# DeltaNet with an MLP on one core: inverse matrices stored turned over, the preparation of four steps moved into the regular loop, and the opening order written anew

## The chip, the cores and the metric

The kernel runs on one core of a Trainium2 chip. The core has five engines with an instruction queue each: TensorE (PE: matmuls and transposes by matmul; its weight loads are shown as PEld), VectorE (DVE), ScalarE (ACT), GpSimd (POOL) and SyncE (SP, which here only issues DMAs). The metric is the time of one execution on the device in microseconds. Every time below without a unit is in microseconds.

## The reference

Two parts, all in f32. The first is DeltaNet, a linear attention with a state, for 4 batches, 8 heads, 768 tokens and a head dimension of 48:

```python
k_n = k / (np.linalg.norm(k, axis=-1, keepdims=True) + 1e-06)
for t in range(S):
    kt, vt, bt = (k_n[:, :, t], v[:, :, t], beta[:, :, t, None])
    y[:, :, t] = np.einsum('bhd,bhde->bhe', q[:, :, t], state)
    v_old = np.einsum('bhde,bhd->bhe', state, kt)
    state = state + bt[:, :, :, None] * np.einsum('bhd,bhe->bhde', kt, vt - v_old)
```

The second is an MLP on the 3072 tokens so made, with 384 features, 2048 hidden units and 384 outputs: `h = x @ w_in`, `g = h * clip(h + 3, 0, 6) / 6`, `out = g @ w_out`. The weights `w_in` and `w_out` arrive as float64, the rest as float32.

## The kernel before, in words

**Steps.** The 768 tokens are cut into N = 24 chunks of 32, called steps here. One step has all batches and heads: 4 × 32 tokens on the 128 partitions, 8 heads side by side. Inside a chunk the recurrence is solved at once: with L the strictly lower part of beta · k kᵀ, one needs the inverse of I + L, a 32 × 32 triangular matrix for each batch and head, 32 of them a step. The steps are grouped: group 0 is step 0, group 1 steps 1 to 4, group 2 steps 5 to 8, group 3 steps 9 to 12, and so on, four steps and so 128 matrices a group.

**What a step runs.** `norms` (a square on ACT or POOL, a sum on DVE, a root on ACT, four small DVE operations; the last writes `inv`, L410) gives the norms of k. `prep(t)` scales k on POOL (kb, L480), makes the masks mb with beta (L458) and bkb (L468) on POOL, turns k and q by eight PE transposes (pt, L496), copies them with ACT (KQ, L504), multiplies them on PE (sc, L517) and masks the products with DVE into L and LB (L528). `chain(t)` is the recurrence: PE multiplies the state with k and q (ks, L776), DVE forms R (L789), PE multiplies R with the inverse X (pz, L797), ACT copies that to Z, PE forms the update of the state (su, L894), and DVE takes it from the state (L909). An output part makes y, turns it on PE (yt, L842), and ACT writes it as xT (L846), the input of the MLP.

**The inverses.** Step 0 alone is inverted by matmuls (`product`: pi, L566, with DVE transposes and sums between). For the other groups DVE transposes L so that each of the 128 matrices lies on one partition (`taken`, A<-L, L448), eliminates in place (pairs of a product pr and a difference A, L729 and L734, 60 operations; items called `i2` and so on), and transposes back (`given`, X<-A, L452). Group 1 eliminates only the two 16 × 16 halves of each matrix (`halves_of`, L700 and L705, 28 operations) and joins them step by step with matmuls (`join`, L654 and DVE's L664 to L672; word `x`).

`problems` says how a matrix of 32 × 32 lies in the 1024 elements of its partition: element (i, c) of the transpose goes to place 32 c + i. `turn` is the view of L or X that the DVE transposes read or write: per element i, all 4 × 8 places (t, h), so that neighbours of one 32-block lie 32 elements, 128 bytes, apart.

**The weights.** The 16 pieces of w_in and w_out of 768 KB are loaded as bit patterns of float64 and converted: four ACT operations a piece for the exponent (`scales`, L335; word `a`), three DVE operations (`convert`, L357, L362, L368; word `c`).

**The MLP.** A block is two steps, 256 tokens; there are 12. `up` is 16 units per block: three matmuls (ph, L948), a relu on ACT (L956, words `r`) and on DVE a minimum and product into g (L959, words `g`). For block 0 it is done for each of its steps apart (words `ua`, `ub`, 128 tokens wide). `down` multiplies g with w_out (po, L988); from block 2 on it is done with seven products for eight (L1053), with DVE sums of g (L1039).

**The order.** The engines take their instructions in the order in which the program issues them, and that order is written by hand. `ORDER` (L22 to L44) is a string of words; each word takes the next item of one generator, and `w*3` three of them: `k`, `q`, `v`, `w` loads of keys, queries, values and weight pieces, `B` beta, `z` and `s` settings (beta turned by L234, then eye, blocks, corner, places, L252), `n` norms, `p` prep, `m` mask, `b` bkb, `x` product or join, `h` chain, `y` output, `i1`, `i2` items of the inverses of groups 1 and 2, `u` MLP units, `e` output stores. Each load is four DMAs of 48 KB on SP's queue. Two PSUM pools turn over in rings, of two and of four tiles.

After ORDER comes the regular part, a loop over t = LS = 5 to 23. Each step takes NU = 15 MLP units, and `plan` says which item of the chain of step t, and of the preparations of later steps, is issued at which unit. `LA` = 6 is how far the preparation is ahead: step t finishes the preparation of t + 6 (`now`) and begins that of t + 7 (`later`). ORDER therefore holds preparations 0 to 10 and the first item of 11. `fill` gives two or three items a unit of the norms or the next group's inverse; the inverse of group g + 1 is begun in the second step of group g (i == 1) at unit 6, and units 6 to 11 of that step take none of it beyond the first.

Of the kernel before, what the change touches and what calls it, by code (L numbers as in the profile page):

```python
# [22 lines left out]
k*3 B k B*3 z n0*3 w z*3 s z q*2 n0 q n0 q v n0 w n0 a p0 a p0 s p0*2 m0 k*2 w p0 a*3 p0 a c a c v  # L23
p0 x0 a c k a x0*4 k a k x0 c k w*2 n1 c a c*2 k a x0 a*2 k a x0 k c*2 x0*2 n1 v c n1 k a q n2 c w
x0 a x0*2 k*2 m1 a*3 n1 s n2 c n1 a*2 x0 n1 c k*2 x0 n1 v x0 b0 n2 p1 c a n2 s b1 q h0 a c*2 h0 c
n2 w n2 a m2 k h0 s n2 q c z k q p1 n4 a y0 a p1 n2*2 p2*2 h0 q a p1 s*2 q*2 n4 p3 w q c n4 p2 c
p1 n4*2 p3 c n4 q*2 n4 b2 c a p2 p3 q*2 p2 p1 a q p2 c q*2 a p2 k p3 a p3 p4*3 q k m3 p4*2 s p1 p3
v p4 c y0 w y0*2 p3 ua m4 p4 ra ua b4 ua i1*6 ra*2 i1 k w ga i1*2 a ga ua ra i1*2 ua ga*2 i1 ra q
ua v ra a ua v i1 ga i1 ra ga ua s q i1*2 ua i1 ga i1 ra*2 ga i1 a i1*3 h1 ua i1 ra ga v ua ra
i1*2 v a ga i1*2 ga ua ra i1*2 ua a ga y1 i1 ua i1 x1 w x2 ra ua x2 x1 x2 ra ga*2 a x1 ra x1 k x1  # L30
ua x3 k x3 c x1 ra h1 y1 c h1*2 v y1 ga y1*2 q x3 c*2 w x3 a*2 y1 ub a v ub c ga h1 c rb*2 ub q rb
x2*2 k gb*2 v h1 ub q gb ub*2 rb c h2 n5 gb rb h2 gb k x2 ub a m5 v rb gb rb ub c gb y2 ub h2 q rb
w ub gb rb v n5 y2 u gb ub x4 a h2 k*2 q rb q n5 k*2 a n5 a k c rb y2 h2 y2 k gb a k n5 a ub gb y2
h2 ub c rb gb h3 rb ub gb v y2 c k q n5 v x3 h3 x3 y3 k*2 w k h3 a h3 b3 n5 u y3 rb x4 y3 a k n5*2
a w gb y3 c ub k n5 y3*2 rb gb c v n5 c u n5 u h3 ru gu a ru n5 a gu p5 h3 n9 x4 v c p5 b5 u p5 u
a*2 q h4 a p6 p5 a p5 x4 u v ru k c u a ru gu y4 n9 b6 x4 m6 v c q h4 k q gu u x4 k y4 p6 p7 u q
k*3 p6 k p7 h4 k n9 a q h4 p8 p7 p5 a c p5 k u n9 k p7 ru gu h4 p6 p7 m7 n9 h4 q b7 q u a c p6 n9
u p8 ru gu u k c k v n9*2 p8 c n9 b8 n9*3 p6 p8 w u n9 p6 c p8 p7 p8 p7 p9 ru m8 u p8 gu u c q ru
ub gu rb y4 v m9 m10 a i2*3 gb i2*2 k u i2 y4 a i2*3 u i2 k i2 v*2 u a ru*2 gu p10 p9 b10 k b9 p9
q i2 u p10 i2*2 u k i2*2 p10 q i2 v q i2 p9 i2 q a gu p9 q i2 u ru i2 q i2*3 u ru i2*3 p9 c v i2*2  # L40
gu u gu i2*3 v p9 i2*2 u q i2 u ru i2 k q*2 i2 k u gu k i2 u q u ru u i2 gu e v p11 y4 e i2*2 ru
i2 k u i2 u gu u p10 e u p10 i2 p10 e i2*4 y4 u q i2*2 k i2 k i2*2 k i2*5 k i2 ru k gu i2 k i2*2
k*2 p10
# [4 lines left out]
def kernel(  # L48
# [395 lines left out]
    def problems(A):  # L444
        return A.rearrange("p (c i) -> p i c", i=C)
# [239 lines left out]
    def halves_of(g):  # L685

        n = 128
        needs(*(("L", first(g) + i) for i in range(size(g))))
        At = work.tile([128, C + 1, C], FP32, name="A", bufs=1)
        flat = At[:].rearrange("p c i -> p (c i)")  # L690
        A = flat[:, 0 : C * C]
        taken(g, A)
        yield
        D2 = flat.rearrange("p (k r) -> p k r", k=2)[:, :, 0 : HC * C]
        D2 = D2.rearrange("p k (c i) -> p k c i", i=C)
        for j in range(1, HC - 1):
            w = HC - 1 - j
            pr = work.tile([128, C * C // 4 - C // 2], FP32, name="pr", bufs=1)
            pv = pr[0:n, 0 : 2 * j * w].rearrange("p (k c i) -> p k c i", k=2, c=j)
            nc.vector.tensor_tensor(  # L700
                out=pv, in0=D2[:, :, j, j + 1 : HC].unsqueeze(2).to_broadcast([n, 2, j, w]),
                in1=D2[:, :, 0:j, j].unsqueeze(3).to_broadcast([n, 2, j, w]), op=ALU.mult,
            )
            yield
            nc.vector.tensor_tensor(  # L705
                out=D2[:, :, 0:j, j + 1 : HC], in0=D2[:, :, 0:j, j + 1 : HC], in1=pv,
                op=ALU.subtract,
            )
            yield
        nc.vector.memset(A[:, 0 : C * C : C + 1], -1.0)  # L710
        yield 1
        given(g, A)
        past.update(("halves", first(g) + i) for i in range(size(g)))
        yield

    def inverse(g):
# [8 lines left out]
        for j in range(1, C - 1):  # L725
            w = C - 1 - j
            pr = work.tile([128, C * C // 4 - C // 2], FP32, name="pr", bufs=1)
            pv = pr[0:n, 0 : j * w].rearrange("p (c i) -> p c i", c=j)
            nc.vector.tensor_tensor(  # L729
                out=pv, in0=A[:, j, j + 1 :].unsqueeze(1).to_broadcast([n, j, w]),  # L730
                in1=A[:, 0:j, j].unsqueeze(2).to_broadcast([n, j, w]), op=ALU.mult,
# [3 lines left out]
                out=A[:, 0:j, j + 1 :], in0=A[:, 0:j, j + 1 :], in1=pv, op=ALU.subtract  # L735
# [426 lines left out]
    LA = 6  # L1162
    LS = G0 + GS
# [10 lines left out]
    def chain_of(t):  # L1174
        return made(("h", t), lambda: chain(t))
# [54 lines left out]
    def do(word):  # L1230
# [10 lines left out]
        else:  # L1241
            name, t = word[0], int(word[1:])
            if name == "p" and t >= LS + LA:
# [5 lines left out]
    with tc.manual_schedule():  # L1249
# [12 lines left out]
        for t in range(LS, N):  # L1262
            g, i = group(t)
            ch, now, later = chain_of(t), prep_of(t + LA), prep_of(t + LA + 1)
# [18 lines left out]
            }  # L1283
            for u in range(NU):
# [3 lines left out]
                if u == 6 and i == 1:  # L1288
# [9 lines left out]
                if i == 1 and 5 < u < 12:  # L1298
                    continue
# [34 lines left out]
```

## Time and profile before

| what | value |
|---|---|
| time, median of 3 runs | 689.57 (689.39 to 689.74) |
| the profiled execution, own time | 690.61 |
| its span in the profile | 688.9 |
| mean granted PE clock in it | 0.99 |
| HBM read, written | 26.84 MB, 4.72 MB |
| PE instructions | 11208 matmuls, 11208 weight loads |

The costliest groups of the page; after the bar stand busy time, the mean of one in ns, and the idle time of the engine just ahead of them with what ended most of it:

```profile
L948 PE MATMUL ph<-xT,w_in 128*128 128x256 f32 (+1 forms) x1248 | 270.0, 369 | 4.2 <-DVE g L959 2.9
...
L959 DVE SCALAR_TENSOR_TENSOR g<-g,ph 128x256 f32<-128x256 f32 (+1 forms) x208 | 81.0, 396 | 106.0 <-ACT g L956 105.8
...
L1053 PE MATMUL po<-w_out,g 128*128 128x192 f32 x640 | 113.3, 328 | 0.0
...
L734 DVE TENSOR_TENSOR A<-A,pr 128x30 f32<-128x30 f32 (+9 forms) x150 | 54.2, 361 | 3.7
L335 ACT ACTIVATE spare<-spare,places 128x768 uint16<-128x768 uint16 (+1 forms) x56 | 52.5, 940 | 4.1 <-DVE places L252 3.3
L729 DVE TENSOR_TENSOR pr<-A 128x30 f32<-128x30 f32 (+9 forms) x150 | 50.3, 335 | 3.0
...
L480 POOL TENSOR_TENSOR kb<-kf,inv 128x384 f32<-128x384 f32 x24 | 21.6, 900 | 158.4 <-DVE inv L410 73.7
```

### The profile page before, as it was taken

To read this page: it belongs to the slowest core of one execution; us is meant where nothing else is said; L and a number is where in the kernel's file an instruction comes from. 1 tells how busy PE (TensorE), PEld (TensorE's weight loads), DVE (VectorE), ACT (ScalarE), POOL (GpSimd) and SP (SyncE) were. 2 spreads that over 40 slices of the span, in tenths; PEclk is the share of its full clock that TensorE was granted. 3 is DMA by queue.
4 is the path that set the end of the run, shared out by engine and by line. 5 is a ranking of instruction groups with operands and counts; after the bars stand their busy time and mean duration, and the time that the engine had idled before them with its cause. 6 is when DMAs were issued, how large, how long until landed. Compare 5 with 4: busy or idle time off the path is not lost.

```text
span 688.9 us, 25309 instructions
## 1 busy us (share of the span) xinstructions
PE 644.7 (94%) x11208; PEld 565.0 (82%) x11208; DVE 464.3 (67%) x1210; ACT 239.1 (35%) x476; POOL 92.9 (13%) x147
## 2 busy tenths in 40 slices
PE   1468799999999999999999999999999999999997
PEld 1357687767678988988988988988988989989997
DVE  4798776799836986845986745985546985445242
ACT  4886378542132232232232232232232132132220
POOL 5063003331501100501100402100000000000000
PEclk9999799999999999999999999999999999999999
DMA  9877026402132030031020030020020020000000
GB/s 236 240 184 183 4 83 134 83 3 58 29 60 46 3 65 9 3 73 33 4 59 14 3 70 2 3 59 2 3 48 2 2 48 2 25 3 1 25 0 24
DMA packets 88494, 33.20 MB, mean 48 GB/s; under 512 B 80160, under 2 KB 83232, under 8 KB 88384
## 3 DMA queue, kind: packets, MB, share of 16 engines
q1 hardware_dynamic: 88128, 31.29, 19.9%
q8 instruction: 88, 1.44, 0.9%
q10 hardware_dynamic: 256, 0.30, 0.2%
q14 instruction: 22, 0.18, 0.1%
HBM read 26.84 MB, written 4.72 MB: 46 GB/s over the span
## 4 chain that ended last, share of the span: by engine, by line
PE 76%; DVE 14%; DMA 4%; issue 2%; SPq 2%; ACT 1%; POOL 0%; DVEq 0%; ACTq 0%
PE ph L948 33%; PE po L1053 21%; PE po L988 5%; PE ks L776 3%; PE pz L797 3%; DVE A L734 3%; PE pt L496 3%; PE su L894 2%; PE py L797 2%; DVE pr L729 2%; DVE g L1039 2%; PE sc L517 2%; DMA vf<-in_v_dram 1%; PE yt L842 1%; DVE R L789 1%
## 5 line engine op out<-in xcount | busy, mean ns | idle before, releaser
L948 PE MATMUL ph<-xT,w_in 128*128 128x256 f32 (+1 forms) x1248 | 270.0, 369 | 4.2 <-DVE g L959 2.9
L948 PEld LDWEIGHTS ph<-xT,w_in 128*128 128x128 f32 x1248 | 220.2, 192 | 33.9 <-DVE g L959 4.7
L956 ACT ACTIVATE g<-ph,halves 128x256 f32<-128x256 f32 (+1 forms) x208 | 94.8, 457 | 201.7 <-PE ph L948 200.9
L959 DVE SCALAR_TENSOR_TENSOR g<-g,ph 128x256 f32<-128x256 f32 (+1 forms) x208 | 81.0, 396 | 106.0 <-ACT g L956 105.8
L1053 PE MATMUL po<-w_out,g 128*128 128x192 f32 x640 | 113.3, 328 | 0.0
L1053 PEld LDWEIGHTS po<-w_out,g 128*128 128x128 f32 x640 | 103.8, 190 | 0.5
L1053 PE MATMUL po<-spare,g 128*128 128x192 f32 x480 | 84.8, 330 | 0.0
L1053 PEld LDWEIGHTS po<-spare,g 128*128 128x128 f32 x480 | 78.1, 190 | 1.8
L1039 DVE TENSOR_TENSOR g<-g 128x256 f32<-128x256 f32 x160 | 65.5, 463 | 0.5 <-PE po L1053 0.5
L734 DVE TENSOR_TENSOR A<-A,pr 128x30 f32<-128x30 f32 (+9 forms) x150 | 54.2, 361 | 3.7
L335 ACT ACTIVATE spare<-spare,places 128x768 uint16<-128x768 uint16 (+1 forms) x56 | 52.5, 940 | 4.1 <-DVE places L252 3.3
L729 DVE TENSOR_TENSOR pr<-A 128x30 f32<-128x30 f32 (+9 forms) x150 | 50.3, 335 | 3.0
L988 PE MATMUL po<-w_out,g 128*128 128x384 f32 x128 | 45.7, 493 | 0.0
L1060 ACT ACTIVATE o<-po 128x192 f32<-128x192 f32 x40 | 13.2, 330 | 88.1 <-PE po L1053 88.1
L480 POOL TENSOR_TENSOR kb<-kf,inv 128x384 f32<-128x384 f32 x24 | 21.6, 900 | 158.4 <-DVE inv L410 73.7
L458 POOL TENSOR_TENSOR mb<-beta_tok,mask 128x256 f32<-128x256 f32 x48 | 34.5, 741 | 47.2 <-DVE LB L528 47.1
L504 ACT ACTIVATE KQ<-pt 128x512 f32<-128x512 f32 x48 | 28.3, 595 | 35.0 <-PE pt L496 34.6
L846 ACT ACTIVATE xT<-yt 128x384 f32<-128x384 f32 x24 | 11.7, 487 | 64.3 <-PE yt L842 64.3
L988 PEld LDWEIGHTS po<-w_out,g 128*128 128x128 f32 x128 | 22.9, 190 | 11.9
L496 PE MATMUL pt<-ident,kb 128*128 128x128 f32 x96 | 16.2, 295 | 14.7 <-POOL kb L480 14.5
L909 DVE TENSOR_TENSOR state<-state,su 128x384 f32<-128x384 f32 x46 | 23.2, 546 | 9.7 <-PE su L894 9.7
L789 DVE SCALAR_TENSOR_TENSOR y<-ks,parity,y 128x192 f32<-128x192 f32 x46 | 17.0, 412 | 17.6 <-ACT y L813 17.6
(109 smaller groups left out, 601.3 us busy)
## 6 DMA issues: line engine op xcount, KB each, us to landing
kf<-in_k_dram SPq DMA_DIRECT2D x96, 48.0 KB, 2.5
qb<-in_q_dram SPq DMA_DIRECT2D x96, 48.0 KB, 2.3
vf<-in_v_dram SPq DMA_DIRECT2D x96, 48.0 KB, 2.1
out_dram<-o SPq DMA_DIRECT2D x92, 48.0 KB, 1.6
spare<-in_moe_w_in_dram SPq DMA_DIRECT2D x4, 768.0 KB, 5.9
w_out<-in_moe_w_in_dram SPq DMA_DIRECT2D x4, 768.0 KB, 5.8
w_out<-in_moe_w_out_dram SPq DMA_DIRECT2D x4, 768.0 KB, 5.8
spare<-in_moe_w_out_dram SPq DMA_DIRECT2D x4, 768.0 KB, 4.6
```

Of the source, the lines that this page charges most:

```text
L335: nc.scalar.activation(out=z, in_=z if n else d.bitcast(I16)[:, :, :, 3], func=func, bias=places[:, n : n + 1], scale=scale,)
L458: nc.gpsimd.tensor_tensor(out=mb[:, e], in0=beta_tok[:, t, e:H:2].unsqueeze(2).unsqueeze(3).to_broadcast([P, NP, 2, C]), in1=mask2[:].unsq ...
L496: nc.tensor.transpose(pt[:, p, :], src[:, 2 * p : 2 * p + 2].rearrange("p e w -> p (e w)"), ident[:])
L729: nc.vector.tensor_tensor(out=pv, in0=A[:, j, j + 1 :].unsqueeze(1).to_broadcast([n, j, w]), in1=A[:, 0:j, j].unsqueeze(2).to_broadcast([n ...
L734: nc.vector.tensor_tensor(out=A[:, 0:j, j + 1 :], in0=A[:, 0:j, j + 1 :], in1=pv, op=ALU.subtract)
L797: nc.tensor.matmul(ps[rows(place(b)), D * h : D * h + D], lhsT=m(h)[rows(b)], rhs=z[rows(b), D * h : D * h + D], start=True, stop=True, sk ...
L948: nc.tensor.matmul(ph[:, cols], lhsT=w_in[:, s, f * 128 : (f + 1) * 128], rhs=xT[:, s, cols], start=(s == 0), stop=(s == NKT - 1),)
L956: nc.scalar.activation(out=g, in_=ph, func=ACTF.Relu, bias=half, scale=1.0 / 6.0)
L959: nc.vector.scalar_tensor_tensor(out=g, in0=g, scalar=1.0, in1=ph, op0=ALU.min, op1=ALU.mult)
L988: nc.tensor.matmul(pos[c][:], lhsT=gs[blk, f // 2][:, f % 2, c * P : (c + 1) * P], rhs=w_out[:, f, :], start=(f == 0), stop=(f == NFC - 1),)
L1039: nc.vector.tensor_tensor(out=A(f, *out), in0=A(f, *a), in1=A(f, *b), op=op)
L1053: nc.tensor.matmul(ps[n][:], lhsT=A(f - f % 2, *a)[:, f % 2], rhs=b[:, f], start=(f == 0), stop=(f == HF - 1),)
```

## The change

Three things are done.

1. `problems` gives element (i, c) the place 32 i + c, so the 1024 elements of a matrix are written by A<-L and read by X<-A in sequence. The L and X sides of the two transposes stay as they were. `halves_of` and `inverse` index A with the two axes exchanged: the same number of operations on the same number of elements.

2. `LE = 4`: ORDER holds preparations 0 to 8 and the first item of 9. The loop makes up for it: at t = 5 it issues 9 and 10 and begins 11, at t = 6 it issues 11 and 12 and begins 13; from t = 7 on it is as before. The additional one (`more`) is taken at units 7, 8 and 10 to 13. The inverse of group 3 is begun at t = 7, unit 0, not at t = 6, unit 6, without the skipped units; those of later groups are begun as before.

3. ORDER is written anew: 786 words' worth of items for 804. The number of MLP units, chain, output and inverse items in it is the same. Among what differs: SP issues eight loads of k and four of q ahead of the first weight piece, where four of k stood ahead of it; the small DVE operations of the first norms stand ahead of the transpose of beta; of group 1 only step 1 is joined between X<-A and the next MLP unit; and parts of the preparations of 5 to 7 stand ahead of the first unit of block 1.

The core of the diff, without the text of ORDER beyond its first lines:

```diff
 ORDER = """
-k*3 B k B*3 z n0*3 w z*3 s z q*2 n0 q n0 q v n0 w n0 a p0 a p0 s p0*2 m0 k*2 w p0 a*3 p0 a c a c v
+k*3 B z k B k*4 B q B n0*7 q*3 w n1 z n1 k s p0 z k z n1 m0 w n1 p0*3 s p0*2 n1*2 z k q n1 k a*3
...
     def problems(A):
-        return A.rearrange("p (c i) -> p i c", i=C)
+        return A.rearrange("p (i c) -> p i c", c=C)
...
             nc.vector.tensor_tensor(
-                out=pv, in0=A[:, j, j + 1 :].unsqueeze(1).to_broadcast([n, j, w]),
-                in1=A[:, 0:j, j].unsqueeze(2).to_broadcast([n, j, w]), op=ALU.mult,
+                out=pv, in0=A[:, j + 1 :, j].unsqueeze(2).to_broadcast([n, w, j]),
+                in1=A[:, j, 0:j].unsqueeze(1).to_broadcast([n, w, j]), op=ALU.mult,
             )
             yield
             nc.vector.tensor_tensor(
-                out=A[:, 0:j, j + 1 :], in0=A[:, 0:j, j + 1 :], in1=pv, op=ALU.subtract
+                out=A[:, j + 1 :, 0:j], in0=A[:, j + 1 :, 0:j], in1=pv, op=ALU.subtract
             )
...
     LA = 6
+    LE = 4
...
-            if name == "p" and t >= LS + LA:
+            if name == "p" and t >= LS + LE:
                 next(prep_of(t), None)
...
-            ch, now, later = chain_of(t), prep_of(t + LA), prep_of(t + LA + 1)
+            ch = chain_of(t)
+            behind = t - LS < LA - LE
+            first_of = t + min(LA, LE + t - LS)
+            now, more, later = (prep_of(first_of + n) for n in range(3))
+            if not behind:
+                more, later = (), more
...
+            if behind:
+                for u in (7, 8, 10, 11, 12, 13):
+                    plan[u] = lambda ch=plan.get(u): (ch and u < 13 and ch(), take(more))
+                plan[14] = lambda: take(later)
+            ready = (2, 0) if behind or i == 2 and t - LS == LA - LE else (1, 6)
...
-                if u == 6 and i == 1:
+                if (i, u) == ready:
...
-                if i == 1 and 5 < u < 12:
+                if i == 1 == ready[0] and 5 < u < 12:
                     continue
```

`halves_of` is changed as `inverse` is. Most lines of the kernel after have numbers lower by one.

## Prediction, on record before the run

> **What bounds it now.** I read the page first: busy times, the 40 slices, the chain that ended last.
>
> ```profile
> PE 644.7 (94%) x11208; PEld 565.0 (82%) x11208; DVE 464.3 (67%) x1210; ACT 239.1 (35%) x476; POOL 92.9 (13%) x147
> ...
> PE   1468799999999999999999999999999999999997
> ...
> DVE  4798776799836986845986745985546985445242
> ...
> PEclk9999799999999999999999999999999999999999
> ...
> PE 76%; DVE 14%; DMA 4%; issue 2%; SPq 2%; ACT 1%; POOL 0%; DVEq 0%; ACTq 0%
> ```
>
> TensorE (PE) is busy for 644.7 of 688.9 us. What it lacks lies in the first seven slices. So I asked for busy times by stage, cut at the first product of step 0 (16.01), the transpose into the matrices of steps 1 to 4 (54.95) and the first unit of block 1 (107.36). Columns: window, length, then busy us of PE, weight load, DVE, ACT and POOL, granted clock, DMA share, GB/s.
>
> ```profile
> 0.00:16.01 16.01, 3.15 (x72) 2.51 (x72) 5.77 (x20) 6.72 (x10) 8.34 (x33) 1.00 0.91 226
> 16.01:54.95 38.94, 22.41 (x867) 19.00 (x867) 32.27 (x73) 33.88 (x49) 14.22 (x25) 0.96 0.84 221
> 54.95:107.36 52.41, 45.19 (x1292) 40.13 (x1292) 41.16 (x114) 31.76 (x67) 2.30 (x5) 0.90 0.36 86
> 107.36:220.63 113.27, 111.66 (x1864) 83.51 (x1865) 83.10 (x193) 44.70 (x83) 33.76 (x42) 1.00 0.28 56
> 220.63:688.90 468.27, 462.32 (x7116) 419.84 (x7114) 301.96 (x812) 122.04 (x270) 34.27 (x44) 1.00 0.10 22
> ```
>
> Before 107.36, PE idles 12.86, 16.53 and 7.22 us, together 36.6; after it 1.6 in one stretch and 6.0 in the other, of which 4.0 are the tail. So from 107 on the kernel is a queue of PE work; every microsecond by which that queue is further on at 107 is one at the end, unless another engine holds PE up later. The stretch 16 to 55 is no PE stretch: ACT is busy for 87% of it, DVE for 83%, DMA for 84%.
>
> The early waits come from the list of instructions in order of time:
>
> ```profile
> 8.49 0.98 DVE L234 STREAM_TRANSPOSE beta_tok<-spare 128x768 f32<-128x768 f32 x1 [2.02 <-DMA qb<-in_q_dram]
> ...
> 11.04 0.97 POOL L480 TENSOR_TENSOR kb<-kf,inv 128x384 f32<-128x384 f32 x1 [6.31 <-DVE inv L410]
> ...
> 16.01 0.42 DVE L528 TENSOR_TENSOR X<-sc,mb 128x256 f32<-128x256 f32 x1 [3.19 <-PE sc L517]
> ```
>
> The first matmul waits for POOL's kb, and kb for DVE's inv. Inv stands in DVE's queue behind the beta transpose, though the root that it needs ended at 6.81 (6.51 plus .30).
>
> **The change by parts.** From the first L1053 on (220.47 before) the two programs give PE the same sequence, and ahead of it the same matmuls in another order. All gain or loss is therefore the time at which PE gets there, plus what the moved work does to the other engines later.
>
> *Start and first inverse.* The new order puts the first norm chain ahead of the beta transpose. From its first reciprocal to kb took .98 (10.06 to 11.04), so kb can start at 6.81 + .98 = 7.8: 3.25 earlier, and the product of step 0 at about 12.8. Against this, weight piece 0 is issued behind twelve 48-KB loads, not four. At .46 each from .80 on that is 6.35 for 2.70; with 5.9 to land, 12.25, where its conversion began at 10.15. ACT loses 2.1 by it, but two KQ copies (.60 each), a square (.52) and a root (.30), 2.0 in all, now precede it: nothing net if the cover holds, 2.1 if it doesn't. DVE's work up to the first A<-L is the same but one L368 (1.0) of the 32.27 in that stretch. I take 2.8 for the first A<-L, bounds 1.0 (a late piece) to 5.0 (the 3.25, the L368 and some of DVE's 6.7 idle): **−2.8**.
>
> *Turned matrices.* Counts and elements of the halves' and the inverse's 88 products stay, only which axis is j and which w; I put them at nothing (the same 58 elements took .21 to .22 as two rows of 29 and as 29 rows of two, so ±.01 an op, ±.3 for the 28 of group 1). Two transposes gain one contiguous side:
>
> ```profile
> L448 DVE STREAM_TRANSPOSE A<-L 128x1024 f32<-128x1024 f32 x6 | 12.6, 2104 | 0.0
> ...
> L452 DVE STREAM_TRANSPOSE X<-A 128x1024 f32<-128x1024 f32 x6 | 12.5, 2081 | 0.2
> ...
> L234 DVE STREAM_TRANSPOSE beta_tok<-spare 128x768 f32<-128x768 f32 x1 | 1.0, 979 | 2.0 <-DMA qb<-in_q_dram 2.0
> ...
> L582 DVE STREAM_TRANSPOSE VY<-VY 128x256 f32<-128x256 f32 x1 | 0.4, 446 | 0.0
> ```
>
> With both sides plain, 512 further elements cost .53 us, 1.04 ns each: 1024 would take 1.25, .85 less than now. One side stays strided by 128 bytes, and no row shows that form, so each saves 0 to .85. For both on the chain of group 1, bounds 0 to 1.7; I take half, −.85. [...]
>
> Between these two transposes DVE gets 9 units' g operations and one L368 where it had 12 g (.28 each): +1.0 − .84 = +.15. Together **−.7**.
>
> *Join of step 1 alone.* After X<-A, one L664 (.45) and 64 small products stand before the next unit, where two and 96 stood (32 took .64): **−1.1**.
>
> *Preparation of steps 5 to 7 as filler.* Seven rows of pt (four transposes, .44) and one sc of .79, 3.9 us of PE work, now stand before the first unit of block 1. If all fell into idle PE time they would be won whole (bound −3.9; there are 7.2 idle in that stretch); if the chain waits behind them, 0. PE's clock was halved where it idled, which limits what fits. Nearest row: a stretch with DVE full and PE half busy (second fence below). **−.5**.
>
> *Steps 9 to 12 moved into the regular part.* They issue per step eight transposes, a sc, two KQ copies, two L528, and POOL's kb (.90), two mb (.74) and bkb, behind k and q loads on SP's queue, which gain lead there (DMA share .28). L of steps 9 to 12 is due at the third inverse, the rest from 257 on; POOL is busy for 33.76 of 113.27 us there, so I cost PE's wait for it at 0; without that cover a prep is 3.2 us of POOL. What it costs is DVE: the third inverse starts at step 7 instead of at unit 6 of step 6, which moves a transpose (2.1) and eight items (.40 each), 5.3 us, from a slack stretch to a full one.
>
> ```profile
> 155.00:172.20 17.20, 17.20 (x189) 12.06 (x187) 15.98 (x43) 3.74 (x8) 2.39 (x3) 1.00 0.28 58
> ...
> 189.40:206.70 17.30, 17.30 (x259) 13.66 (x258) 5.70 (x15) 6.38 (x13) 0.83 (x1) 1.00 0.31 60
> 223.90:241.10 17.20, 17.20 (x369) 16.38 (x361) 16.06 (x43) 3.48 (x8) 3.29 (x4) 1.00 0.01 3
> ```
>
> Third window: DVE 16.06 of 17.20. It has 1.14 free, 1.7 in the 25.6 us of step 7. The inverse itself isn't late (done at 263.93, first used at 282.56), but PE's units may wait for their g behind it. That wait was .64 at 254.21. Bounds −.64 (gone) to +3.6 (5.3 − 1.7); I take one more such wait: **+.6**.
>
> *Second inverse.* Between its two transposes DVE gets two more g (.40), three norm sums (.53), four small ones (.2) and two state sums (.52), less four L528 (.41): +2.6, in the stretch of the first window above, 15.98 of 17.20. It is paid from the lead that the start gives: 0 in the forecast, +2.6 at worst.
>
> *Clock.*
>
> ```profile
> 72.00:74.00 2.00, 1.02 (x64) 0.91 (x61) 2.00 (x7) 0.00 (x0) 0.00 (x0) 0.50 0.00 0
> 82.00:84.00 2.00, 2.00 (x68) 1.78 (x69) 1.97 (x6) 0.65 (x2) 0.00 (x0) 0.50 0.04 8
> ```
>
> The granted clock was .50 from 70.8 to 77.2 and from 81 to 84.2. The second stretch has a busy PE, so it costs about half its 3.2 us, 1.6; filler may prevent it or another may come: 0 ± 1.6. [...]
>
> *Sum.* −2.8 − .7 − 1.1 − .5 + .6 = −4.5. The profiled execution took 690.61 (span 688.9, 1.7 around it), 1.04 above the median 689.57. 690.61 − 4.5 = 686.1 by its own time, **685.1** beside the median.
>
> **Rivals.**
> *Gain used up* (.12). DVE paces from 138 on: for it speak 15.98 of 17.20 and the +2.6; against it that PE waited only .58 from 137.8 to 155. Then the transpose X<-A of steps 5 to 8 stays at 170 or later, the lead is lost there, and the time is 688.6 to 689.6.
> *Slower* (.14). VectorE is the bound in steps 7 and 8: the lead is eaten as in the first rival, and the moved 5.3 less 1.7 free make PE wait 3.6 for g, behind inverse items. 689.57 + 3.6 = 693.2. It decides once DVE has no idle time left from 223 to 255. Against it: PE has several units of lead there, since its wait was .64 at most.
> *Clock or a late weight* (.08). One more stretch like 81 to 84 (+1.6), a weight piece 2.1 late, DVE's +2.6 in the second inverse, and none of the −4.5: up to 691 or so, half of it within the band below.
> The change can fail to do what it says only in the preparations, which can't come late for PE; that is part of the first.
>
> **Numbers.** The forecast case has .66, all of it faster. A measurement can tell 0.2%, 1.4 us, from no change: faster below 688.2, slower above 691.0. The first rival and half of the third are the same: .16; the second and the other half are slower: .18. Low end: 685.1 with the first inverse's 2.2 to its bound and half of the filler's 3.9 beyond mine, 681.0 (.05 below). High end 691.5, which leaves out the slower rival.
>
> **What would show it.** Right: first matmul at 8 to 9 us, first product's X at 12.5 to 13, first A<-L at 51 to 53, transposes of 1.3 to 2.1, first unit of block 1 by 105 in spite of 3.9 us more work done before it, no PE wait above 1 us from 138 on. Wrong: A<-L after 54, ACT idle for weight piece 0 beyond 12.5, a clock of .50 longer than 12 us in all, or PE waiting for g in steps 7 and 8.

## The result, and the profile after

The changed kernel took 690.04 (median; 686.79 to 694.99), the kernel before, timed beside it, 690.66 (688.35 to 693.15). The ratio is 0.9992, with a 95% interval of 0.9974 to 1.0011: no difference that this measurement can tell, where 4.5 us less were forecast. The profiled execution of after took 688.24 with a span of 686.5, so 2.4 less span than before's 688.9; it lies 1.8 below its own median, and two further profiled executions of the same kernel took 690.39 and 687.97. What is read from one profile below is read with that in mind.

The page of after, the lines that answer to those shown of before:

```profile
PE 647.2 (94%) x11208; PEld 567.8 (83%) x11208; DVE 467.8 (68%) x1210; ACT 238.9 (35%) x476; POOL 95.2 (14%) x147
...
PE   2668989999999999999999999999999999999997
...
DVE  5898776888746997846985745985546985445242
...
PEclk9977899999999999999999999999999999999999
...
PE 73%; DVE 12%; DMA 7%; issue 3%; ACT 2%; SPq 1%; POOL 0%; DVEq 0%; ACTq 0%; POOLq 0%
```

PE idles 39.3 (686.5 − 647.2) for 44.2: 4.9 less. But it is busy 2.5 longer for the same 11208 matmuls, and its clock shows two slices of 7 and one of 8 where before had one of 7. DMA and "issue" have 10% of the chain that ended last, for 6%.

Busy times by stage, cut at the same four events (columns as before):

```profile
0.00:12.46 12.46, 3.15 (x72) 2.51 (x72) 5.07 (x24) 4.56 (x9) 8.13 (x33) 1.00 0.67 157
12.46:49.55 37.09, 23.08 (x875) 18.99 (x875) 33.29 (x69) 35.12 (x49) 14.22 (x22) 0.91 0.96 242
49.55:110.88 61.33, 52.10 (x1435) 46.06 (x1436) 47.73 (x125) 39.28 (x79) 11.84 (x18) 0.89 0.41 100
110.88:218.40 107.52, 106.38 (x1712) 80.07 (x1713) 78.41 (x181) 37.92 (x72) 26.37 (x33) 1.00 0.29 56
```

The first product's X is written 3.55 earlier (12.46 for 16.01), and the first A<-L starts 5.4 earlier (49.55 for 54.95). From 218.40 to the end it is 468.1 for 468.27: unchanged. So in this profile most of the lead of 5.4 went in the third window. In the two further profiles of after the first A<-L starts at 52.59 and 51.85, so the lead there is 2.4 and 3.1. In the third window POOL is busy for 11.84 where it was for 2.30, and PE idles 9.2 of 61.33.

Three rows of after, the first two from the list in order of time, the third from the groups:

```profile
8.51 1.11 PE L495 MATMUL pt<-ident,kb 128*128 128x128 f32 x4 [8.51 <-POOL kb L479]
...
12.46 0.42 DVE L527 TENSOR_TENSOR X<-sc,mb 128x256 f32<-128x256 f32 x1 [2.15 <-PE sc L516]
```

```profile
L447 DVE STREAM_TRANSPOSE A<-L 128x1024 f32<-128x1024 f32 x6 | 11.8, 1962 | 0.0
```

The start did what the change says. The transposes take 1.96, not 2.10: .13 less each, not the .85 that stood in the sum.

What ended PE's waits, by kind (columns: total, number, longest), from 0 to 125 of after:

```profile
PE ks L775 <- issue: 2.9, 2, 1.7
...
PE sc L516 <- issue: 2.9, 2, 1.7
...
PE py L796 <- issue: 1.4, 1, 1.4
```

and of before:

```profile
PE pz L797 <- issue: 1.0, 1, 1.0
...
PE sc L517 <- issue: 0.6, 1, 0.6
```

"Issue" is a wait in which nothing that the program shows was missing. All such waits of PE come to 2.6 in before and to 11.2 in after, one of which (1.5 at a ph, put down to an ACT operation long done) is counted in by its place. What they are, the experiments tell.

**A measure for the lead.** A moment minus the PE work issued ahead of it (each kind of instruction at its usual duration) is the time that PE has lost by then, idle or slowed. Other choices of the usual duration move the differences between the two orders by up to 3 at yt 2, but by less than .4 at yt 6, and the differences between rows of one order by some tenths. Taken at ACT's copies behind an output's transposes (yt of step t) or behind the inverse product (pz of step t):

| profiled execution | yt 0 | pz 1 | yt 2 | yt 3 | yt 6 | own time |
|---|---|---|---|---|---|---|
| before | 39.0 | 43.9 | 47.1 | 47.3 | 53.1 | 690.61 |
| after | 35.4 | 41.8 | 45.2 | 45.8 | 50.8 | 688.24 |
| after, second | 37.0 | 43.4 | 47.2 | 48.6 | 52.6 | 690.39 |
| after, third | 36.6 | 42.1 | 44.9 | 45.5 | 50.3 | 687.97 |
| e3_pool_held | 38.2 | 42.0 | 45.4 | 46.0 | 51.3 | 688.98 |
| e18_held_piece_later | 36.9 | 41.3 | 43.0 | 43.6 | 48.4 | 685.79 |

Own time less the value at yt 6 is 637.4 to 637.8 in all six. The time of these six is therefore set by what is lost up to step 6, and what differs lies ahead of it.

### The profile page after: what moved, and what is told of

Same layout as the page of the kernel before. It is cut to its first block, busy times and chain, and to the rows that moved or that the text cites. A ratio compares the mean times of both kernels' runs of the same rounds, so it can differ in the third digit from the quotient of the medians.

```text
span 686.5 us, 25308 instructions
## 1 busy us (share of the span) xinstructions
PE 647.2 (94%) x11208; PEld 567.8 (83%) x11208; DVE 467.8 (68%) x1210; ACT 238.9 (35%) x476; POOL 95.2 (14%) x147
## 3 DMA queue, kind: packets, MB, share of 16 engines
q1 hardware_dynamic: 88128, 31.29, 20.5%
q8 instruction: 88, 1.44, 0.9%
## 4 chain that ended last, share of the span: by engine, by line
PE 73%; DVE 12%; DMA 7%; issue 3%; ACT 2%; SPq 1%; POOL 0%; DVEq 0%; ACTq 0%; POOLq 0%
PE ph L947 33%; PE po L1052 21%; PE po L987 4%; PE ks L775 3%; PE py L796 2%; PE su L893 2%; PE pz L796 2%; DVE g L1038 2%; DMA w_out<-in_moe_w_in_dram 2%; DVE pr L728 2%; DVE A L733 2%; PE sc L516 2%; PE pt L495 2%; DMA spare<-in_moe_w_in_dram 2%; DMA qb<-in_q_dram 1%
## 5 line engine op out<-in xcount | busy, mean ns | idle before, releaser
L733 DVE TENSOR_TENSOR A<-A,pr 128x30 f32<-128x30 f32 (+9 forms) x150 | 52.2, 348 | 3.4
L479 POOL TENSOR_TENSOR kb<-kf,inv 128x384 f32<-128x384 f32 x24 | 23.0, 958 | 155.2 <-PE pt L495 69.9
L775 PEld LDWEIGHTS ks<-state,KQ 64*64 64x64 f32 x1472 | 24.3, 136 | 10.2 <-issue 9.0
L845 ACT ACTIVATE xT<-yt 128x384 f32<-128x384 f32 x24 | 11.7, 486 | 57.3 <-PE yt L841 57.3
L775 PE MATMUL ks<-state,KQ 64*64 64x48 f32 x1472 | 27.7, 222 | 3.7 <-issue 2.9
```

What stands on the lines that cost most here:

```text
L733: nc.vector.tensor_tensor(out=A[:, j + 1 :, 0:j], in0=A[:, j + 1 :, 0:j], in1=pv, op=ALU.subtract)
L775: nc.tensor.matmul(ph[y][c, e, D * p : D * p + D], lhsT=KQ[r, p * B // 2 + b // 2, 2 * y : 2 * y + 2, :].rearrange("k y c -> k (y c)"), rh ...
```

## The experiments

Theories at the start: **T**, turning the matrices over costs DVE what the start gains; **P**, POOL's work, which the new order puts beside DVE's elimination, slows it; **I**, PE runs out of instructions at places that depend on their count and on DMA traffic; **L**, the lead of the start is lost again on the way, whatever made it.

### The changed kernel twice more

Two further profiled executions of after, unchanged, to see what one profile can tell.

> The kernel after once more, unchanged, for a second profile: its executions spread from 686.8 to 695.0 and the first profile fell at 688.2. Theory (supply): the waits for instructions stand at the same counts of matmuls as in the first profile (126 to 128 records apart), and a later end comes from their lengths, which follow the DMA traffic at that moment. Rival (clock): the waits are of the same length, and the 3.4-us windows at half clock fall on other work; their number or place then accounts for the difference, at up to 1.7 us a window.

> As the look before it: a third profile of the same kernel after, with the same two theories. If its end lies beyond 690, the stage in which it is late tells which: waits for instructions before 55 us, or half-clock windows.

They are the second and third rows of after above: 690.39 and 687.97. The sum of the issue waits hardly differs (11.3 and 12.0), the loss at yt 3 does (48.6 and 45.5): the places of the waits belong to the kernel, their cost to the execution. The clock differs too: the profile shows .50 for 20.5 in the first, 23.9 in the second and 13.7 in the third, and only the second has a stretch of it at 100.3. Whether that or the lengths of single waits (one of 3.72 at 50.32 in the second) made the second late wasn't tried apart.

### One part alone: the matrices, the start, the third inverse

*e1*: before with `problems`, `halves_of` and `inverse` turned over, ORDER and loop as they were. *e2*: after with these three turned back.

> The kernel before with the turned matrices alone (problems, the halves' and the inverse's indices). The prediction's working gave each of the twelve transposes 0 to 0.85 us less; the profile after shows 1.96 to 1.99 for 2.08 to 2.10. Theory: the side that stays strided sets the transpose's time; the transposes take 1.97, the 88 products and differences are unchanged to 0.01 us each, and the time stays within 1 us of before (ratio 0.9985 to 1.0015). Rival: the turned operations carry the change's gain or loss; then the ratio is beyond 0.997 or 1.003.

> The kernel after with the matrices turned back, so that only the order and the loop are new. Theory: the transposes go back to 2.10, and the time is that of after to 1 us (688 to 692). If the turning were what cost the gain, this run would be about 4 us faster than after, near the 685 of the prediction.

e1: 689.95, ratio 0.9991 (0.9978 to 1.0005). Transposes 1.94 to 1.99, the stretch between the two of group 1 11.89 for 11.97. e2: 691.02, ratio 1.0008 (0.9987 to 1.0029), transposes 2.07 to 2.12. T falls: the turning is worth some tenths, and with it taken back the time doesn't fall.

*e5*: before, with only DVE's order of the first norms changed. *e11*: the same with the matrices turned over.

```diff
-k*3 B k B*3 z n0*3 w z*3 s z q*2 n0 q n0 q v n0 w n0 a p0 a p0 s p0*2 m0 ...
+k*3 B k B*3 z n0*7 w z*3 s z q*2 q q v w a p0 a p0 s p0*2 m0 ...
```

> The kernel before with one thing of the new order: the four small DVE operations of the first norms ahead of the transpose of beta, nothing else moved on any engine. The prediction's step: the first product's X comes 3.2 us earlier (16.0 to 12.8) and the first transpose of L 2.8 earlier, and the lead lasts, so the time falls by about 2.8 us (686 to 688.5). Rival (another engine paces the stretch to 55 us): ACT was busy 87% of it, and PE's instructions come in loads that can't follow each other at will; then X comes 3.2 earlier, the first transpose of L less than 1.5 earlier, and the time falls by less than 1.5.

> The kernel before with the two parts of the change that gave something there: the first norms' four operations ahead of the transpose of beta (alone 0.9988) and the turned matrices (alone 0.9991), with before's own order, preparation depth and third inverse. If they add, 0.9979, about 689.2, which is as fast as the whole change or faster (0.9992), and the rest of the change, the new order behind the start and the later preparations, then gave nothing in sum or cost about 1 us. If only one of them is real, 0.9990.

e5: 689.66, 0.9988 (0.9977 to 0.9998). In its profile the first product's X is 1.9 earlier (14.07) and the first A<-L 2.4 (52.55); the median fell by about .8. e11: 689.55, 0.9969 (0.9955 to 0.9982). By the ratios e11 is about 1.6 faster than after, with an uncertainty of 1.6. So a few moved words and the turning give at least as much as the whole change; the rest of it gave nothing in sum that can be told.

*e6*: before, with the inverse of group 3 begun at t = 7, unit 0.

```diff
-                if u == 6 and i == 1:
+                ready = (2, 0) if t < LS + 2 or i == 2 and t == LS + 2 else (1, 6)
+                if (i, u) == ready:
...
-                if i == 1 and 5 < u < 12:
+                if i == 1 == ready[0] and 5 < u < 12:
```

> The kernel before with the inverse of group 3 begun at step 7, unit 0, and nothing else changed. The prediction's step costed this at +0.6 us, bounds -0.6 to +3.6, by PE waits for g in steps 7 and 8. In the profile after, PE idles 0.2 us from 220 to 290 where before it idled 0.6, so the theory now is that it costs nothing: the time within 1 us of before, PE's wait for g in steps 7 and 8 under 0.7. If VectorE were the bound there, PE would idle 2 us or more from 220 to 290.

690.42, 0.9992 (0.9978 to 1.0007): the later inverse costs nothing that can be told.

### POOL beside the elimination

*e3*: after, with the mask of step 6 (and so the POOL work behind it) held until DVE's elimination of group 1 is done. A one-column POOL copy that reads A behind DVE's last write to it makes it wait (it ran at 63.89).

```diff
     def mask(t):
+        if t == 6:
+            nc.gpsimd.tensor_copy(out=hold[:], in_=held[0])
...
+        held.append(A[:, 0:1])
```

> The kernel after, with GpSimd's mask of step 6 and two bkb behind it held until the elimination of group 1 is over (a one-column copy that reads the matrices after their last write). In the profile after, these three stand beside four DVE operations of the elimination that took 0.56 to 0.91 us for 0.21 to 0.25, 1.9 us in all. Theory: GpSimd slows DVE's two-operand SBUF work; the stretch between the two transposes of group 1 goes from 13.6 to 11.7 us and X comes 1.9 earlier. The time falls by 1.5 to 1.9 us if that lead reaches the end, and by less than 0.5 if PE loses it again to its own waits (clock or instruction supply) before 110 us. Rival: the four slow operations are a sampling accident and the stretch stays at 13 or more.

688.50, 0.9959 (0.9938 to 0.9980). The stretch from A<-L to X<-A is 11.71, for 13.58 in after and 11.97 in before. DVE and POOL of after, in order of time:

```profile
53.60 0.56 DVE L699 TENSOR_TENSOR pr<-A 128x72 f32<-128x72 f32 x1
...
54.98 0.91 DVE L699 TENSOR_TENSOR pr<-A 128x88 f32<-128x88 f32 x1
```

```profile
52.89 1.19 POOL L457 TENSOR_TENSOR mb<-beta_tok,mask 128x256 f32<-128x256 f32 x2
...
54.96 0.83 POOL L467 TENSOR_TENSOR bkb<-kb,beta_tok 128x384 f32<-128x384 f32 x1
```

and DVE operations of the same sizes in e3, with POOL idle:

```profile
56.48 0.23 DVE L704 TENSOR_TENSOR pr<-A 128x72 f32<-128x72 f32 x1
...
57.02 0.25 DVE L704 TENSOR_TENSOR pr<-A 128x88 f32<-128x88 f32 x1
```

The product of 88 elements takes .91, in effect as long as the bkb (.83) that runs beside it, where it takes .25 alone. The POOL rows are no longer than elsewhere (bkb .83 at 54.96 here, .83 at 65.18 in e3). P holds, for 1.9 of the stretch. DVE's products are as short in the other runs with POOL held, and the stretch is 11.7 in five of these seven; it is 12.34 in e12 and 13.87 in e18, where DVE waits for g of the MLP units (1.25 at 57.84 in e18, behind a wait of PE for instructions of 3.60). By the two ratios the held kernel is about 2.3 faster than after, with an uncertainty of about 1.9. The profiles alone don't show that: at yt 6 e3 has lost 51.3, the three executions of after 50.8, 52.6 and 50.3.

A transpose in before, which reads one input, kept its 2.10 at 54.95 beside an mb that ran from 54.98 to 56.17; a product of 72 elements there took .66 at 64.15, beside a bkb from 63.79 to 64.72, for .23 at 58.02.

### PE's instructions

The profile's list of DMA queues has, in before and after, this row:

```profile
q8 instruction: 88, 1.44, 0.9%
```

1.44 MB in 88 transfers are 16 KB each. PE has 22,558 instructions in the trace of before and 22,556 in that of after, which is 256.3 a transfer; so I take one transfer to carry 256 of them, about 128 matmuls with their weight loads. Counted in each trace, every long "issue" wait of PE stands at an instruction whose number is 193 or 194 modulo 256, and PE goes on 1.2 to 1.8 after the end of one of these transfers. That gives I its form: PE waits at a fixed place of the count when the transfer came late.

Two transfers were late with next to no other traffic in their way. In before PE passed one such place at 69.66; the next transfer began at 70.63, with the DMA engines busy for .10 of the 3 us ahead of it, and took 1.1. PE came to the next place at 72.27, waited .98 and went on at 73.25, 1.5 after the end of the transfer; it passed the two places 3.6 apart. In e18 a wait of .59 at 83.22 came the same way, with the places 4.0 apart and the engines at .13. So in these two cases dense small matmuls were enough for waits of .98 and .59; each of the 73 waits longer than about 1 in all the traces follows a transfer ahead of which the DMA engines were busy for .4 or more of 3 us, and each of the 21 over 2 one with .76 or more. The sums of these waits:

| old order | us | new order | us |
|---|---|---|---|
| before | 2.6 | after (three executions) | 11.2, 11.3, 12.0 |
| e1, e5 | 2.2, 1.7 | e2, e3 | 8.0, 12.9 |
| e6, e11 | 2.1, 1.8 | e4, e7, e8 | 7.3, 14.8, 9.6 |
| e15 | 3.1 | e12, e13, e14 | 8.4, 12.5, 10.5 |
| | | e16, e17, e18 | 13.8, 6.9, 6.1 |

*e4*: after, with 32 products of 32 × 32 ahead of the first transpose, in PE's idle time, which shift the count by 64 matmuls (the trace shows two for a product), half a transfer. *e8*: the same in e3.

```diff
+        for _ in range(32):
+            nc.tensor.matmul(
+                dummy[0:32, 0:32], lhsT=ident[0:32, 0:32], rhs=ident[0:32, 0:32], start=True, stop=True,
...
```

> The kernel after with 32 small matmuls of 32 x 32 put ahead of the first transpose, where PE waits for kb anyhow (8.5 us idle, they take about 1.5): 64 matmul records. Theory (supply): PE's instructions arrive in loads of 16 KB, one for about 128 matmul records with their weight loads, and PE waits for a load wherever small matmuls use one up sooner than the next arrives. In after those waits stand at 27.6, 33.0, 43.3, 47.3, 51.7, 71.5 and 96.9 us, 9.7 us in all to 2.6 before, 126 records or a multiple apart. Moved by half a load they fall elsewhere: the list changes, and the time moves by more than 1 us, in either direction, with the sum of these waits. Rival (clock or DVE sets it): the waits stay where they were, and the time is that of after to 1 us.

> Both changes that helped, on the kernel after: GpSimd's three operations held until the elimination of group 1 is over, and the 32 small matmuls ahead of the first transpose. Held alone gave 688.5 (0.9959 of before), shifted alone 689.4 (0.9977). If they are two mechanisms at two places, the ratio is their product, 0.9936, about 686.5. If both only return the same lead, it is 0.996.

e4: 689.37, 0.9977 (0.9956 to 0.9998); the waits moved to other work and their sum fell from 11.2 to 7.3. The time is about 1 below after, within what can't be told. e8: 688.70, 0.9966 (0.9948 to 0.9985), no better than e3, though its waits fell from 12.9 to 9.6. The places of the waits follow the count; that the shift is worth time isn't shown.

*e7*: after, with the products sc of steps 2 and 3 done twice (128 matmuls more, 1.6 of work). *e13*: after, with three large products at each of the same two places. *e14*: e3 without the odd heads' sc of steps 1 to 4 (112 matmuls fewer net). *e15*: before without them.

```diff
-        for p in range(NP):
+        for p in list(range(NP)) * (2 if t in (2, 3) else 1):
```

> The kernel after with the 32 small matmuls sc of steps 2 and of 3 issued twice (the second time they write the same values): 128 more matmul records, one more load of instructions, in the stretch before the first transpose of L. Their PE time is 0.8 us a step, 1.6 in all, twice that at half clock. Theory (supply): PE can use up 128 records in 1.6 us there, but the loads follow each other only every 4 to 6 us, so one more load makes the chain before 52 us 2 to 5 us later, and one more wait 'issue' stands in it. Rival (PE is idle for 14 of the 37 us there, and DVE and ACT pace it): the first transpose of L and the time move by less than 1.

> The counterpart of issuing sc of steps 2 and 3 twice: in the same two places of the kernel after, three 128 x 128 matmuls of the identity each, into columns of sc that nothing reads. That is as much PE time or more (12 records of 0.14 at full clock, 1.7 us in all, for 1.6) in 12 records instead of 128. Theory (supply): what cost 3.2 us there was the extra load of instructions, so this costs less than 1.5 against the kernel after (690.0): under 691.5. Rival (PE time): the same 3 us again, 692.5 or more.

> The kernel after with GpSimd's operations held, and in steps 1 to 4 the 16 small matmuls of the odd heads' sc replaced by two 128 x 128 matmuls of the identity: the odd heads' products of these steps are left out. PE time stays (32 records of 0.0124 are 0.40, 4 of 0.14 are 0.57 a step), 112 records fewer, nearly one load of instructions. Theory (supply): the chain before 55 us gets one load shorter, 1.5 to 4 us against the held kernel's 688.5: 684.5 to 687. Rival (the lead is lost to the clock or to DVE alone): no change, 688 to 689.5.

> The same replacement in the kernel before (the odd heads' products of steps 1 to 4 left out): 112 matmul records fewer at the same PE time. Before has 2.6 us of waits for instructions where after has 9.7. If the new order ran into the supply and the old one had not yet, this gains less than 1 us against before; if both are as much bound by it, it gains as much as the new order does.

e7: 693.24, 1.0041 (1.0026 to 1.0056), about 3.4 more than after for 1.6 of work; its waits are 14.8. e13: 691.91, 1.0009 (0.9985 to 1.0034), about 1.2 more than after, between what the two theories expect and too wide to decide. e14: 689.39, 0.9971 (0.9952 to 0.9990), no gain over e3, against what I expected: the second transpose of group 1 was 1.9 earlier (62.62), but a wait of 3.66 stood at 75.2 instead. e15: 690.34, 0.9987 (0.9969 to 1.0004), under 1 as expected for the old order. So fewer instructions are no cure by themselves; the waits move.

*e12*: e3, with ten products of 128 × 128 ahead of the first transpose, against the slow PE at the start (1.11 for four transposes that later take .66).

> The kernel after with GpSimd's three operations held, and ten 128 x 128 matmuls of the identity ahead of the first transpose, in PE's idle 8.5 us: about 5.7 us of PE work at half clock. In the profiles the first four transposes take 1.11 us where later ones take 0.66, though the clock row shows full speed there, so PE starts at half clock. Theory (clock): the first transposes then take 0.66 and X of step 0 comes 0.8 to 1.3 earlier, at about 11; the time falls by 0 to 1 us against the held kernel's 688.5, since ACT paces the stretch behind it. Rival: the transposes stay at 1.1 because they are slow for another reason.

689.24, 0.9948 (0.9919 to 0.9978). The first four transposes took .66 instead of 1.11, and X came at 11.41. In time it can't be told from e3. The clock shown in this run is .50 from 9.24 to 29.72, so it tries faster first transposes alone. Without the products PE stays slow for longer than that: in before four transposes of the same kind still took 1.11 at 40.26, though the clock is shown as 1.00 there, and .66 at 43.83:

```profile
40.26 1.11 PE L496 MATMUL pt<-ident,kb 128*128 128x128 f32 x4
43.83 0.66 PE L496 MATMUL pt<-ident,kb 128*128 128x128 f32 x4 [1.02 <-POOL kb L480]
```

**What makes a transfer late.** In e3 the trace shows an instruction transfer that began at 94.55, in the middle of a 768-KB weight piece that SP issued at 90.73. Three experiments keep e3 and are to move that piece, number 13. When its issue waits, the 48-KB loads of q and v behind it on SP's queue wait too (in e17, below, PE waited 4.24 for one of them), so what moves is the piece together with these.

*e16*: its word `w` behind five loads of 48 KB. *e17*: a one-column DVE write to its landing place, late in DVE's queue, so that the piece waits for it. *e18*: the same write at the state update of step 2, a little later than the piece's usual start:

```diff
+        if word == "D":
+            needs(("seen", 10, 0), ("seen", 10, 1))
+            nc.vector.memset(homes[5][:, 0:1], 0.0)
```

> The kernel after with GpSimd's operations held, and the load of weight piece 13 (768 KB, issued at 90.7 us) put behind the next five loads of 48 KB on SP's queue, 2.4 us later. In all profiles of the new order PE waits 1.7 to 2.4 us at matmul record 2002 (about 97 us), and the load of instructions that ends that wait starts at 94.5, under a DMA share of 0.90 in the 3 us ahead of it; loads at 77 to 89, with the DMAs idle, cause no wait. Theory (the instruction load queues behind the weight piece): the wait at record 2002 falls below 0.7, R of step 3 comes about 1 us earlier, and the time falls by 0 to 1 against the held kernel's 688.5, more than which five rounds may not show. Rival (density of the matmuls alone): the wait stays at 1.7.

> The same question, with the load of weight piece 13 now tied to VectorE's work: a one-column memset of its landing place is put behind the R and the second conversion step of about 98 to 104 us, and the load must wait for it, so it can't be issued at 90. Theory (the instruction load queues behind the weight piece): with the DMAs nearly idle from 92 to 96, the load of instructions that started at 94.5 starts before 94, and the wait at record 2002 falls from 1.7 to below 0.7. Rival (density of the matmuls alone): it stays at 1.5 or more. The piece comes 13 us later, so the end may be later by a few us; only the wait is asked for.

> The kernel after with GpSimd's operations held, and weight piece 13 held by 2 to 3 us only: the one-column memset of its landing place stands behind the state update at 92 to 93 us, so the load is issued at about 93.3 for 90.7. In the run before this one the piece came at 100.6, the load of instructions started at 91.3 for 94.5, and the wait of 1.7 us at record 2002 was gone. Theory (the instruction load queues behind the weight piece): the wait at record 2002 is gone or below 0.7 here too, time lost by the third output is 1 to 3 us less than the held kernel's 45.4, and, the piece being only 2.6 late, the time is 0 to 1.7 us below the held kernel's 688.5. Rival: the wait returns at the next load of instructions, and the time stays at 688 to 689.

e16 did not move what it was to move: the piece went out at 89.8, since it starts when its landing place comes free, and the wait stayed 1.95 (689.44, 0.9978, 0.9954 to 1.0001). e17 issued the piece at 100.63; the instruction transfer began at 91.25 and the wait was gone, with 42.1 lost at yt 2 for 45.4; but the loads of q behind the piece were then too late, PE waited 4.24 for one of them up to 105.61, and at yt 3 48.8 were lost (689.28 in its one execution). e18: 686.00 (683.11 to 690.91), 0.9932 (0.9908 to 0.9956), the lowest of all and below both kernels. PE and SP's queue in e3, in order of time:

```profile
94.35 1.03 PE L781 MATMUL ks<-state,KQ 64*64 64x48 f32 x54
97.05 0.37 PE L781 MATMUL ks<-state,KQ 64*64 64x48 f32 x10 [1.68 <-issue]
```

```profile
90.73 0.38 SPq L309 DMA_DIRECT2D w_out<-in_moe_w_out_dram  x1
```

and in e18:

```profile
93.63 1.43 PE L780 MATMUL ks<-state,KQ 64*64 64x48 f32 x64
```

```profile
92.47 0.38 SPq L308 DMA_DIRECT2D w_out<-in_moe_w_out_dram  x1
```

In e3 the 64 products of one line are cut after 54, with nothing missing but instructions. With the piece issued 1.7 later (92.47), the transfer began at 92.06 for 94.55 and the 64 run through. PE had passed the place before at 91.61 for 92.33, so the transfer began .45 behind PE for 2.22: 1.8 of the 2.5 are the traffic's, the rest is that PE was earlier. The loss from pz 1 to yt 2 is 1.7 for 3.4. So I holds at this place, and what delayed the transfer there was the traffic ahead of it, the piece and the loads behind the piece. The whole gain of e18 isn't its doing: of the 2.9 by which it leads e3 at yt 6, .7 stand at pz 1 already, and its waits ahead of that differ as well (3.60 at 54.94 for 1.23; 3.23 at 45.29 in e3 alone). By the ratios e18 is about 1.9 below e3, with an uncertainty of 2.2 (not told apart), and about 4.1 below after, with one of 2.1.

## Why the prediction was wrong

The time lies in the range, but the forecast of a clear gain failed. Step by step:

- **Start and first inverse, −2.8: right.** X −3.55 (−3.2 said). The first A<-L is 5.4 earlier in the first profile of after, a little past the bound of 5.0, but 2.4 and 3.1 in the other two. e1 and e6, whose start is that of before, have it at 53.50 and 53.42; the means of three profiles each are 53.96 and 51.33, so 2.6. The cover for the later weight piece 0 held: ACT began on it at 12.11.
- **Turned matrices, −.7: the step that failed first.** The stretch between group 1's transposes grew from 11.97 to 13.58, +1.6. Two things were wrong in it. The transposes give .13 each, not half of .85: nearer to the lower bound of 0 than to what I took. And POOL had no place in this step: its work was weighed once, for the preparations moved into the regular part, and "cost at 0" because PE doesn't wait for POOL there. What the new order put beside the elimination (third window, POOL 11.84 for 2.30) made DVE wait. e3 shows it: 1.9 of the stretch.
- **Join of step 1 alone, −1.1: about right, by one pair of profiles.** In e3, where the stretch is again as long as before (11.71), the loss from yt 0 to pz 1 is 3.8 for 4.9, some .3 of it from the stretch.
- **Preparations as filler, −.5: didn't show.** The first unit of block 1 came at 110.88, not by 105. With about 4 more work done before it, that is about 107 for 107.36: of a lead of 5.4 about half a us was left there. Before loses more than after behind this point; by yt 6 the difference is 2.3.
- **Third inverse, +.6, and second, 0: no cost.** From 110.88 to 218.40 PE idles 1.1, and e6 shows nothing. VectorE as the bound, the mechanism of the first two rivals, didn't come.
- **Clock, 0 ± 1.6: inside its bounds, by an estimate.** Ahead of the tail the clock is shown as .50 for 20.5 in after (34.2 to 41.1, 51.3 to 58.1, 68.4 to 75.2) and for 13.6 in before (50.0 to 53.4, 70.5 to 77.3, 80.7 to 84.1). The prediction had the last two of before alone, so its sign, more than 12, was met by before itself. Both sums leave out the start, where the clock is shown as 1.00 but four transposes took 1.11, as they do in the stretch of .50 at 36.85: up to 29.07 in after and up to 40.26 in before. The traces' first record of the clock is at 30.81 and at 43.16. If all ahead of it was slow, the slow time is 51.3 in after and 56.8 in before, and PE was busy for 30.8 and 28.0 of it. Half of the 2.8 more is 1.4 of the 2.5 by which PE was busy longer, as an estimate. The six stretches of .50 in before and after are 3.41 or 6.83 long, and in the 3.41 ahead of each PE was busy for 1.56 to 2.27. What brings such a stretch about, and whether filler prevents one, no run shows; whether PE's waits for instructions had a part in these wasn't tried apart.
- **What the sum lacked.** The sentence "all gain or loss is therefore the time at which PE gets there" was right: own time less the loss at yt 6 is the same in all six rows of the table. But the sum reckoned that time from data alone. PE's supply of instructions, 2.6 in before and 11.2 in after, was in no term. That this costs PE time is shown at one place (e3 against e18, 1.7 from pz 1 to yt 2) and supported by e7. It isn't shown that the whole 8.6 more is lost time: some waits fall where PE would have waited for data, and e2, with 8.0, is no faster than after.

So a gain was there at the start, 2.4 to 5.4, and in the median all but some tenths of it was given back in the next 60 us: 1.9 of the stretch to POOL beside the elimination, 1.7 by the trace to one instruction transfer behind weight traffic (in time not told apart), and the rest to further such waits and to the clock, whose shares stay open. Open too is why executions of the new order spread so widely (686.79 to 694.99, for 688.35 to 693.15 of before): the three profiled ones differ by up to 3.1 at yt 3, with nearly the same sum of waits.

## What to carry to other kernels

Price a moved operation on the engine beside which it lands, not only on those that wait for its result: a POOL operation of .83 beside small two-input DVE operations turned .25 into .91. When an order is rewritten and PE is the bound, count where PE's instruction blocks end and what large transfers are under way there, since here each long "issue" wait in the profile was such a block come late, and one in e3 cut the 64 products of one line after 54. And when a lead is forecast at the start, follow it stage by stage by moment less work done, in more than one profile; here that showed that all that differs is settled by step 6.

## What the runs showed of the hardware that was not expected

- PE's waits for instructions stood at 193 or 194 modulo 256 of its instruction count, lasted up to 3.9 (in e7), and ended 1.2 to 1.8 after a 16-KB transfer. In e3 against e18 a 768-KB piece and the loads behind it put the start of such a transfer back by about 1.8 (2.22 behind PE's passing of the place before, for .45). With the DMA engines nearly idle waits were rare and short: none in e3 from 77 to 89, .98 in before at 73.25, .59 in e18 at 83.22.
- At the start of after PE ran slowly though the granted clock is shown as 1.00: four transposes took 1.11 at 8.51, and in e12 .66 at 8.29, with ten products ahead of them. In before they took 1.11 up to 40.26.
- The DVE transposes of 1024 elements took 1.96 (A<-L) and 1.97 (X<-A) in after, with one side in sequence and the other strided, and 2.10 and 2.08 in before, with both strided: 6% less.
